# Attention and a gated expert layer on one core: queries and keys of the two heads on even and odd partitions, and every row block stored with its pair

## The chip, the cores and the metric

The kernel runs on one core of one Trainium2 chip. The metric is device time in microseconds (us) of one execution. A profile is one execution taken by the hardware profiler; its times are counted from the start of its span, which is the stretch from the first to the last instruction. TensorE is written PE, its weight load PEld, VectorE DVE, ScalarE ACT, GpSimd POOL and SyncE SP. SPq is the queue of instructions on SP, from which nearly all transfers are issued.

## The reference

The first half is attention inside chunks of 64 rows (8 batches, 8 heads, 576 rows of 64 numbers); the second half sends each of the 4608 rows of 512 numbers to one of 8 experts and keeps 80 rows for each.

```
scores = scale * q_c @ k_c^T              # per chunk of 64 rows
attn   = exp(scores - max); attn /= sum + 1e-9
x      = (attn @ v_c) as rows [4608, 512]
logits = x @ w_gate                       # 8 experts
e      = argmax(logits); gate = softmax(logits)[e]
for each expert: keep the 80 rows with the largest gate
    out[row] = gate * (relu(x[row] @ w1[e]) @ w2[e])
```

All other rows of the output are zero.

## The kernel before

**Stage one, attention.** The rows are cut into 36 blocks of 128 rows, two chunks of 64 each; two blocks make a pair, so there are 18 pairs (`n`), and four blocks make a tile `T` of 9. The loop over `n` is written out by hand: in step `n` PE does the scores of pair `n` (`scores`, tile `s`), turns the finished rows of pair `n-3` (`xtrans`, tile `px`), multiplies the probabilities of pair `n-2` with the values (`values`, tile `o`), turns the probabilities of pair `n-1` (`probs`, tile `pt`), and in even steps does the gate products (`gate_mm`) and, from step 8 on, a count (`tally`). DVE takes maxima and differences of pair `n` and then divides pair `n-2` (`divide`), which writes the finished rows into a tile of SBUF; `store` writes them to the scratch tensor `xs` in HBM.

**Queries and keys.** For each block, `load_qk` fills one of six buffers `qb` of 128 partitions and 1536 columns with two transfers of 64 partitions and 1024 columns (256 KB). One head lies on partitions 0 to 63, columns 0 to 1023; the other on 64 to 127, columns 512 to 1535. Columns 512 to 1023 are then the stationary operand, and columns 0 to 511 and 1024 to 1535 the moving one; the quarters that no head fills are set to zero once, at the start. So one matmul with 128 rows of contraction does both heads. The values go into six buffers `vb` by two transfers each of 130 KB (`load_v`), one head on the even partitions and the other on the odd ones: `vbufs[i % NBV][h:P:2, h]`.

**Rows kept on the chip.** Tiles 0, 2 and 4 (`KEEP`) are written into `kept`, which lies in the two weight buffers that the second expert's weights get later; the others into `x`, of which there are two. The kept tiles are stored whole (1 MB each) in steps 15, 16 and 17 (`DEFER`), after the last load of queries and keys. The others are stored pair by pair, right behind their division.

**The order of transfers.** SP issues transfers in program order, one after the other. Each waits for its buffer to be free and for the transfer issued eight before it to have landed. In steps 15 to 19 (`EARLY`) the weights of experts 0 and 1 are loaded in pieces of 1 MB; the last two wait for a small copy on POOL (L639).

**Stage two, choice of rows.** Behind the loop come the last pairs and gates, the threshold of each expert, and the list of rows. POOL then gathers 128 rows of `xs` at a time into `xgc` (L179), six gathers.

**Stage three, experts.** Two matrix products for each gathered group (`hc` L204, `yc` L237), with the weights of the other six experts and the zero rows of the output on the queue beside them.

Of the kernel before, what the change touches and what calls it, by code (L numbers as in the profile page):

```python
# [8 lines left out]
F32 = mybir.dt.float32  # L9
# [8 lines left out]
P = 128  # L18
# [8 lines left out]
DM = 512  # L27
# [9 lines left out]
LG = NT - 1  # L37
HOT = 8
OB = 171
KEEP = (0, 2, 4)  # L40
DEFER = {15: [0], 16: [2], 17: [4]}
LATER = [[(2, 1), (3, 0), (3, 1)], [(0, 2), (4, 0), (5, 0), (1, 2)], [(4, 1), (5, 1), (2, 2)], [(6, 0), (6, 1), (3, 2), (4, 2), (7, 0)], [(7, 1), (5, 2), (6, 2), (7, 2), (8, 2)], [], [], []]

EARLY = {15: [0], 16: [1], 17: [2, 3], 18: [4], 19: [5]}
# [13 lines left out]
def attention_moe(ctx: ExitStack, tc: tile.TileContext, qk, vv, wg, w1, w2, cap, cst, out):  # L58
# [3 lines left out]
    wp = ctx.enter_context(tc.tile_pool(name="weights", bufs=2))  # L62

    xs = dp.tile([NT * 512, DM], F32, name="xs")
# [219 lines left out]
    with ExitStack() as actx:  # L284
        gk = actx.enter_context(tc.tile_pool(name="gating", bufs=2, side="right"))
        wk = actx.enter_context(tc.tile_pool(name="work", bufs=2))
# [10 lines left out]
            return small[:, turn[0], 0:a * b].rearrange("p (a b) -> p a b", b=b)  # L297

        TT = {}
        kept = []  # L300
        QKV = {}
        XT = {}
        U = {}
# [8 lines left out]
        def pops(k):  # L312
            for _ in range(k):
                step_one(gates)
# [8 lines left out]
        def load_qk(i, eng=nc.sync):  # L323

            d = QKV["qk", i] = qbufs[i % (2 * NB)]
            for h in range(2):
                eng.dma_start(d[64 * h:64 * h + 64, 512 * h:512 * h + 1024],
                              qk[i // 2, i % 2, 64 * h:64 * h + 64])

        vbufs = [wk.tile([P, 2, VW], F32, name=f"vb{j}", tag=f"vb{j}", bufs=1)  # L330
# [2 lines left out]
        def load_v(i):  # L333
            for h in range(2):
                nc.sync.dma_start(vbufs[i % NBV][h:P:2, h], vv[i // 2, i % 2, h])  # L335

        def scores(n):
            d = U[n] = {}
            ps = d['s'] = ps1.tile([P, 2, 512], F32, name=f"s{n}", tag="o" if n == 1 else "s")
            for t in range(2):  # L340
                t8 = QKV["qk", 2 * n + t].rearrange("p (w a u s) -> p w a u s", w=3, a=4, u=2)
                for pr in range(4):
                    for u in range(2):
                        nc.tensor.matmul(  # L344
                            ps[64 * u:64 * u + 64, t, P * pr:P * pr + P].rearrange(
                                "p (h k) -> p h k", h=2),
                            lhsT=t8[:, 1, pr, u, :], rhs=t8[:, 0:3:2, pr, u, :],
                            start=True, stop=True)
# [31 lines left out]
        def values(i, tag=None):  # L380
            n, t = divmod(i, 2)
            T, r = divmod(i, 4)
            d = U[n]
            if r == 0:
                if T in KEEP:
                    k, j = divmod(KEEP.index(T), 2)
                    if j == 0:
                        kept.append(wp.tile([P, 8, DM], F32, name=f"kept{k}", tag=f"w{k + 1}"))
                    TT[T] = kept[k][:, 4 * j:4 * j + 4]
                else:  # L390
                    TT[T] = wk.tile([P, 4, DM], F32, name=f"x{T}", tag="x")
            v = vbufs[i % NBV].rearrange("p h (a u x) -> p h a u x", a=4, u=2)
            if tag is None:
                if t == 0:
                    d['o'] = ps1.tile([P, 3 * 512], F32, name=f"o{n}", tag="o")
                k0, po = 4 * t, d['o']
            else:
                k0, po = 0, ps1.tile([P, 2 * 512], F32, name=f"o{i}", tag=tag)
                U[i, 'o'] = po
            for pr in range(4):  # L400
                c, o = 64 * (4 * t + pr), OB * (k0 + pr)
                for u in range(2):
                    nc.tensor.matmul(  # L403
                        po[64 * u:64 * u + 64, o:o + 130].rearrange(
                            "p (h x) -> p h x", h=2),
                        lhsT=d['pT'][:, u, c:c + 64], rhs=v[:, :, pr, u, :],
                        start=True, stop=True)
# [11 lines left out]
                TT[T][:, r:r + nt, :].rearrange("p r (k h e) -> p (r k) h e", k=4, h=2),  # L419
                pov[..., 0:64], rc[:, :, :, None].to_broadcast([P, k, 2, 64]), op=ALU.mult)  # L420

        def store(n, nt=2):
            T, r = divmod(2 * n, 4)
            if T == 8:
                for u in range(2):
                    nc.sync.dma_start(
                        xs.rearrange("(b s) d -> s b d", s=576)[
                            512:576, 2 * r + u:2 * r + 4:2, :],
                        TT[T][64 * u:64 * u + 64, r:r + 2, :])
            else:  # L430
                nc.sync.dma_start(
                    xs[T * 576:T * 576 + 512].rearrange("(c p) d -> p c d", p=P)[:, r:r + nt],
                    TT[T][:, r:r + nt])

        def xtrans(n, tag="tp"):
            T, r = divmod(2 * n, 4)
# [26 lines left out]
        def gate_sum(T, queue):  # L463
            pm = bank([P, 4, 32])
            nc.tensor.transpose(pm.rearrange("p c e -> p (c e)"), U.pop(('lt', T)), ident)
            gate(4 * T, 4, pm[:, :, 0:NE], queue)
# [177 lines left out]
        with tc.manual_schedule():  # L644
            warm = gk.tile([P, 2 * P], BF16, name="warm", tag="lv", bufs=LV)
            nc.vector.memset(warm, 0.0)
            for j, qb in enumerate(qbufs):
                eng = nc.gpsimd if j == 1 else nc.vector
                eng.memset(qb[64:P, 0:512], 0.0)
                eng.memset(qb[0:64, 1024:1536], 0.0)  # L650
                if j < 2:
                    load_qk(j, (nc.sync, nc.scalar)[j])
            nc.scalar.dma_start(ident, cst[:, C_ID:C_ID + P])
# [5 lines left out]
            def warm_up(n):  # L659
                for j in range(n):  # L660
                    nc.tensor.matmul(pw, lhsT=warm[:, 0:P], rhs=warm, start=True, stop=True)
# [21 lines left out]
            def late_constants():  # L683
                for dst, c0, w in ((io_b, C_IO, 2 * P), (tr_b, C_TR, P)):
                    nc.scalar.copy(dst, ct[:, c0:c0 + w])
                io_h = S['io_h'] = gk.tile([P, P, HOT], BF16, name="io_h", tag="io_h", bufs=1)
                nc.gpsimd.tensor_copy(io_h, io_b[:, P:2 * P, None].to_broadcast([P, P, HOT]))
                nc.gpsimd.tensor_copy(capf, capi)
                nc.gpsimd.tensor_scalar(capc, capf[:, 0:1], 0.0, 4294967296.0,
                                        op0=ALU.is_lt, op1=ALU.mult)  # L690
                nc.gpsimd.tensor_tensor(capt, capf[:, 0:1], capc, op=ALU.add)
                nc.gpsimd.tensor_scalar(capc, capf[:, 1:2], 4294967296.0, None, op0=ALU.mult)
                nc.gpsimd.tensor_tensor(capt, capt, capc, op=ALU.add)
                nc.gpsimd.tensor_scalar(slot_oob, ct[:, C_SL:C_SL + NR], capt, BIG,
                                        op0=ALU.is_ge, op1=ALU.mult)

            for n in range(NPAIR):
                odd = n % 2
                if n == 2:
                    late_constants()  # L700
                scores(n)
                if n + NB < NPAIR:
                    load_qk(2 * (n + NB))
                    if n < 2:
                        load_qk(2 * (n + NB) + 1)
                if n >= 5 and odd:
                    gate_sum((n - 5) // 2, gates)
                if n >= 3:
                    xtrans(n - 3)
                if n >= 2:  # L710
                    for t in range(2):
                        values(2 * (n - 2) + t)
                        if n - 2 + NBV // 2 < NPAIR:
                            load_v(2 * (n - 2) + t + NBV)
                        if t == 0 and n + NB < NPAIR:
                            load_qk(2 * (n + NB) + 1)
                if n >= 1:
                    probs(n - 1)
                if n == 1:
                    warm_up(8)  # L720
                if n >= 7 and odd:
                    for j in range(2 * n - 14, 2 * n - 10):
                        signs(j)
                if n >= 8 and not odd:
                    tally(2 * n - 16, 4)
                if n >= 4 and not odd:
                    gate_mm((n - 4) // 2)
                    gate_copy((n - 4) // 2)
                maxima(n)
                minus(n)  # L730
                if n >= 2:
                    divide(2 * (n - 2), 2)
                    if (n - 2) // 2 not in KEEP:
                        store(n - 2)
                for T in DEFER.get(n, ()):
                    store(2 * T, 4)
                if n >= 8 and not odd:
                    left_add(2 * n - 16)
                if odd:
                    pops(6 if n >= 7 else 4)  # L740
                else:
                    pops(len(gates) - 2)
                if n == NPAIR - 2:
                    own_counts()
                for k in EARLY.get(n, ()):
                    early_weights(k)
# [335 lines left out]
```

## Time and profile before

| what | value |
| --- | --- |
| time, median of 3 runs | 274.38 us (274.06 to 275.83) |
| time of the profiled execution | 277.03 us |
| its span | 275.2 us |
| PE busy, DVE busy | 232.4 us, 119.0 us |
| moved by DMA | 84.73 MB, mean 308 GB/s |
| HBM read, written | 64.00 MB, 20.45 MB |

The profiled execution is 1.0% longer than the median. Mean rates hide that the rate of the DMA engines is not the same in the three stages; the rows further below take it stage by stage.

### The profile page before, as it was taken

How to read it: one execution, taken by the hardware profiler on the slowest of the kernel's cores; microseconds unless marked ns; L12 is line 12 of the kernel's file. 1: busy time of each engine (PE TensorE's matmuls, PEld its weight loads, DVE VectorE, ACT ScalarE, POOL GpSimd, SP SyncE). 2: the span in 40 equal slices, each digit the busy share in tenths (PEclk: the TensorE clock that was granted, in tenths of full speed). 3: DMA queues.
4: the chain of work that ended last, by engine and by line, in shares of the span. 5: the costliest groups of instructions: out<-in, count | busy, mean ns of one | idle time of the engine just before them, and what ended most of it. 6: DMA issues, size and time to landing. Idle time of an engine off the chain costs nothing.

```text
span 275.2 us, 7328 instructions
## 1 busy us (share of the span) xinstructions
PE 232.4 (84%) x3117; PEld 149.7 (54%) x3117; DVE 119.0 (43%) x263; ACT 66.5 (24%) x115; POOL 57.0 (21%) x167
## 2 busy tenths in 40 slices
PE   6773989979788977978868885899999999999990
PEld 4763778968667866766756574234333433333320
DVE  6545366876574846665735846011111211212110
ACT  1012123453251625352614410112020201101000
POOL 8003000121122222222373845300000000000081
PEclk9599799999999999999979779599999999999996
DMA  7998999999999999999999999999999999999431
GB/s 157 237 255 220 233 239 238 274 257 260 232 239 284 288 230 215 276 271 272 365 394 402 409 411 415 393 396 393 409 413 405 407 415 409 416 395 409 182 133 69
DMA packets 35718, 84.73 MB, mean 308 GB/s; under 512 B 4000, under 2 KB 4128, under 8 KB 35680
## 3 DMA queue, kind: packets, MB, share of 16 engines
q1 hardware_dynamic: 34416, 80.73, 93.0%
q0 software_dynamic: 960, 2.88, 2.7%
q10 hardware_dynamic: 304, 0.59, 1.0%
q8 instruction: 27, 0.44, 0.7%
q14 instruction: 11, 0.09, 0.1%
HBM read 64.00 MB, written 20.45 MB: 307 GB/s over the span
## 4 chain that ended last, share of the span: by engine, by line
PE 51%; DMA 39%; SPq 3%; POOL 3%; issue 2%; POOLq 0%; DVE 0%
DMA qb<-in_qk 24%; PE hc L204 16%; PE yc L237 15%; DMA vb<-in_vv 5%; PE o L403 5%; PE s L344 5%; DMA xs<-kept 4%; DMA w<-in_w 4%; DMA xgc<-xs,gic 2%; PE hpc L222 2%; SPq L335 2%; PE pt L369 2%; PE px L369 1%; PE xpc L192 1%; PE small L455 1%
## 5 line engine op out<-in xcount | busy, mean ns | idle before, releaser
L344 PE MATMUL s<-qb 128*64 128x128 f32 x576 | 42.3, 298 | 21.7 <-DMA qb<-in_qk 20.0
L344 PEld LDWEIGHTS s<-qb 128*64 128x64 f32 x576 | 35.6, 150 | 27.0 <-issue 22.4
L204 PE MATMUL hc<-w,xtc 128*32 128x512 f32 x384 | 45.6, 618 | 0.0
L237 PE MATMUL yc<-w,htc 128*32 128x512 f32 x384 | 42.3, 592 | 0.0
L403 PE MATMUL o<-vb,pT 128*64 128x130 f32 x576 | 38.0, 283 | 3.3 <-DMA vb<-in_vv 2.6
L354 DVE TENSOR_REDUCE mx<-s 128x16 f32<-128x1024 f32 x18 | 22.0, 1225 | 36.8 <-PE s L344 36.7
L403 PEld LDWEIGHTS o<-vb,pT 128*64 128x64 f32 x576 | 33.1, 139 | 4.8 <-issue 3.7
L237 PEld LDWEIGHTS yc<-w,htc 128*32 128x32 f32 x384 | 12.4, 110 | 28.3 <-issue 28.3
L204 PEld LDWEIGHTS hc<-w,xtc 128*32 128x32 f32 x384 | 12.6, 113 | 27.3 <-issue 26.7
L446 ACT COPY xT<-px 128x1024 f32<-128x1024 f32 x17 | 17.2, 1013 | 42.3 <-PE px L369 42.3
L378 ACT ACTIVATE pT<-pt 128x1024 f32<-128x1024 f32 x18 | 18.4, 1023 | 32.1 <-PE pt L369 32.1
L256 POOL DMA_INDIRECT out<-ysc,to x6 | 6.0, 993 | 88.5 <-SPq L933 86.1
L359 DVE TENSOR_TENSOR sm<-s,mx 128x1024 f32<-128x1024 f32 x18 | 22.1, 1228 | 0.6
L209 ACT ACTIVATE hsc<-hc 128x512 f32<-128x512 f32 x6 | 3.6, 597 | 65.3 <-PE hc L204 65.3
L242 DVE TENSOR_SCALAR ysc<-yc,gatec 128x512 f32<-128x512 f32 x6 | 4.5, 751 | 33.5 <-PE yc L237 33.5
L418 DVE TENSOR_TENSOR x<-o,rc 128x1024 f32<-128x1024 f32 (+1 forms) x14 | 15.0, 1072 | 0.5
L211 DVE TENSOR_SCALAR hsc<-hc 128x512 f32<-128x512 f32 x6 | 4.1, 691 | 25.2 <-PE hc L204 25.2
L520 POOL TENSOR_SCALAR u<-sx 128x4 f32<-128x4 f32 x8 | 1.6, 195 | 62.1 <-DVE sx L519 38.9
L369 PE MATMUL pt<-ct,sm 64*128 64x64 f32 x288 | 12.8, 229 | 1.2 <-ACT pT L378 1.2
L226 DVE COPY htc<-hpc 128x512 f32<-128x512 f32 x6 | 4.2, 692 | 22.0 <-PE hpc L222 22.0
L369 PEld LDWEIGHTS pt<-ct,sm 64*128 64x128 f32 x288 | 10.3, 139 | 4.3 <-issue 3.0
L545 ACT ACTIVATE lv<-io_b,bo 128x256 bf16<-128x256 bf16 x29 | 12.5, 497 | 0.4 <-DVE bo L526 0.4
(136 smaller groups left out, 233.8 us busy)
## 6 DMA issues: line engine op xcount, KB each, us to landing
w<-in_w SPq DMA_DIRECT2D x12, 2048.0 KB, 18.8
qb<-in_qk SPq DMA_DIRECT2D x70, 256.0 KB, 6.7
vb<-in_vv SPq DMA_DIRECT2D x72, 130.0 KB, 6.6
out<-zero SPq DMA_DIRECT2D x9, 1024.0 KB, 16.3
w<-in_w SPq DMA_DIRECT2D x8, 1024.0 KB, 12.6
xs<-x SPq DMA_DIRECT2D x10, 512.0 KB, 6.5
xs<-kept SPq DMA_DIRECT2D x3, 1024.0 KB, 8.8
xs<-x SPq DMA_DIRECT2D x4, 256.0 KB, 10.7
```

The costliest lines, as they stand in the source:

```text
L204: nc.tensor.matmul(h[o:o + 32, :], lhsT=xT[r][:, b, o:o + 32], rhs=getw(groups[r][g])[0][:, b, 512 * f:512 * f + 512], start=(b == 0), sto ...
L237: nc.tensor.matmul(y[o:o + 32, :], lhsT=hT[r][c // 4][:, c % 4, o:o + 32], rhs=getw(groups[r][g])[1][:, c, :], start=(c == 0), stop=(c == ...
L256: i = nc.gpsimd.indirect_dma_start(out=out, out_offset=bass.IndirectOffsetOnAxis(ap=to, axis=0), in_=ys, in_offset=None, bounds_check=NT * ...
L344: nc.tensor.matmul(ps[64 * u:64 * u + 64, t, P * pr:P * pr + P].rearrange("p (h k) -> p h k", h=2), lhsT=t8[:, 1, pr, u, :], rhs=t8[:, 0:3 ...
L354: nc.vector.tensor_reduce(d['mx'], d['s8'], axis=AX.X, op=ALU.max)
L359: nc.vector.tensor_tensor(d['sm'].rearrange("p c k h -> p h c k"), d['s8'], d['mx'][:, :, :, None].to_broadcast([P, 2, 8, 64]), op=ALU.sub ...
L369: nc.tensor.transpose(pm[:, u, 64 * c:64 * c + 64], src(c)[rows], ident[rows, rows])
L378: nc.scalar.activation(d['pT'], pt, AF.Exp, scale=0.125)
L403: nc.tensor.matmul(po[64 * u:64 * u + 64, o:o + 130].rearrange("p (h x) -> p h x", h=2), lhsT=d['pT'][:, u, c:c + 64], rhs=v[:, :, pr, u, ...
L418: nc.vector.tensor_tensor(TT[T][:, r:r + nt, :].rearrange("p r (k h e) -> p (r k) h e", k=4, h=2), pov[..., 0:64], rc[:, :, :, None].to_br ...
L446: nc.scalar.copy(dst, pm)
L545: nc.scalar.activation(lv, io_b, AF.Sign, bias=bo[:, rt:rt + 1], scale=-1.0)
```

## The change

Queries and keys of one head go to the even partitions and those of the other to the odd ones, as the values do already; what is in HBM and the columns stay as they were. Since the empty quarters now lie on every second partition, the zeros are written over all 128 partitions of the two column ranges before the loads, so the first load of each buffer writes over zeros and waits for them. No tile is kept: all nine go through the two buffers `x`, and all 18 pairs are stored behind their division, 512 KB at a time.

```diff
-KEEP = (0, 2, 4)
-DEFER = {15: [0], 16: [2], 17: [4]}
...
             for h in range(2):
-                eng.dma_start(d[64 * h:64 * h + 64, 512 * h:512 * h + 1024],
+                eng.dma_start(d[h:P:2, 512 * h:512 * h + 1024],
                               qk[i // 2, i % 2, 64 * h:64 * h + 64])
...
             if r == 0:
-                if T in KEEP:
-                    k, j = divmod(KEEP.index(T), 2)
-                    if j == 0:
-                        kept.append(wp.tile([P, 8, DM], F32, name=f"kept{k}", tag=f"w{k + 1}"))
-                    TT[T] = kept[k][:, 4 * j:4 * j + 4]
-                else:
-                    TT[T] = wk.tile([P, 4, DM], F32, name=f"x{T}", tag="x")
+                TT[T] = wk.tile([P, 4, DM], F32, name=f"x{T}", tag="x")
...
                 eng = nc.gpsimd if j == 1 else nc.vector
-                eng.memset(qb[64:P, 0:512], 0.0)
-                eng.memset(qb[0:64, 1024:1536], 0.0)
+                eng.memset(qb[:, 0:512], 0.0)
+                eng.memset(qb[:, 1024:1536], 0.0)
...
                     divide(2 * (n - 2), 2)
-                    if (n - 2) // 2 not in KEEP:
-                        store(n - 2)
-                for T in DEFER.get(n, ()):
-                    store(2 * T, 4)
+                    store(n - 2)
```

The order of instructions on PE and ACT is the same in both kernels; on DVE and POOL only the memsets have another shape; on SP six stores are added and three taken out. The names in the rows are tiles with a buffer number; `waits` names the counters that an instruction waits for, `DMAHW` for an earlier transfer, `DVE`, `Pool` and `PE` for work of that engine.

SP at the start of the program, before:

```order
L327 DMA qb_99<-in_qk 64x1024 x2
L327 DMA qb_101<-in_qk 64x1024 x2
L327 DMA qb_102<-in_qk 64x1024
L327 DMA qb_102<-in_qk 64x1024 [waits DMAHW0_49]
L335 DMA vb_105<-in_vv 64x520 [waits DMAHW1_49,DVE_49]
```

The same place on SP after the change:

```order
L324 DMA qb_99<-in_qk 64x1024 [waits DVE_49] x2
L324 DMA qb_101<-in_qk 64x1024 [waits DVE_49] x2
L324 DMA qb_102<-in_qk 64x1024 [waits DVE_49]
L324 DMA qb_102<-in_qk 64x1024 [waits DMAHW0_49,DVE_49]
L332 DMA vb_105<-in_vv 64x520 [waits DMAHW1_49,DVE_49]
```

Nothing moved, but the loads of queries and keys now wait for DVE's memsets of their buffers.

SP in the middle of the loop, from the loads of the first reused buffers on, before:

```order
L335 DMA vb_105<-in_vv 64x520 x2
L327 DMA qb_104<-in_qk 64x1024 x2
L335 DMA vb_106<-in_vv 64x520 x2
L327 DMA qb_99<-in_qk 64x1024 x2
L335 DMA vb_107<-in_vv 64x520 x2
L327 DMA qb_100<-in_qk 64x1024 x2
L335 DMA vb_108<-in_vv 64x520 x2
```

The same place on SP after the change:

```order
L332 DMA vb_105<-in_vv 64x520 x2
L324 DMA qb_104<-in_qk 64x1024 x2
L332 DMA vb_106<-in_vv 64x520 x2
L422 DMA xs<-x_299 128x2x512
L324 DMA qb_99<-in_qk 64x1024 x2
L332 DMA vb_107<-in_vv 64x520 x2
L324 DMA qb_100<-in_qk 64x1024 x2
L332 DMA vb_108<-in_vv 64x520 x2
L422 DMA xs<-x_299 128x2x512
```

A store that waits for DVE's division now stands ahead of the next pair's loads in every step, where before it stood there only for tiles that were not kept.

SP at the end of the loop, before:

```order
L431 DMA xs<-x_1668 128x2x512
L431 DMA xs<-kept_299 128x4x512
L640 DMA w_0_1875<-in_w 128x2x1024
L335 DMA vb_109<-in_vv 64x520 x2
L335 DMA vb_110<-in_vv 64x520 x2
L431 DMA xs<-x_1914 128x2x512
L431 DMA xs<-kept_299 128x4x512
```

The same place on SP after the change:

```order
L422 DMA xs<-x_1675 128x2x512
L631 DMA w_0_1881<-in_w 128x2x1024
L332 DMA vb_109<-in_vv 64x520 x2
L332 DMA vb_110<-in_vv 64x520 x2
L422 DMA xs<-x_1920 128x2x512
```

The stores of the kept tiles are gone from between the last loads of values.

## Rows read from the trace of the kernel before

**Rows 1.** The chain that ended last, from the page: shares by engine, by line.
```profile
PE 51%; DMA 39%; SPq 3%; POOL 3%; issue 2%; POOLq 0%; DVE 0%
DMA qb<-in_qk 24%; PE hc L204 16%; PE yc L237 15%; DMA vb<-in_vv 5%; PE o L403 5%; PE s L344 5%; DMA xs<-kept 4%; DMA w<-in_w 4%; DMA xgc<-xs,gic 2%; PE hpc L222 2%; SPq L335 2%; PE pt L369 2%; PE px L369 1%; PE xpc L192 1%; PE small L455 1%
```

**Rows 2.** List of waits, whole span: total us, times, longest us.
```profile
PE s L344 <- DMA qb<-in_qk: 20.0, 12, 4.7
```

**Rows 3.** Stretches: length, busy of each engine, clock granted, DMA share, GB/s last.
```profile
11.80:12.80 1.00, 1.00 (x13) 1.00 (x12) 0.73 (x1) 0.00 (x0) 0.00 (x0) 0.50 1.05 193
12.80:13.80 1.00, 1.00 (x14) 1.00 (x12) 0.96 (x2) 0.00 (x0) 0.00 (x0) 0.50 1.07 376
14.00:18.00 4.00, 3.23 (x50) 2.67 (x48) 3.01 (x3) 1.02 (x1) 0.00 (x0) 0.96 1.07 229
28.00:128.00 100.00, 87.22 (x1630) 75.15 (x1627) 64.36 (x117) 39.04 (x61) 16.00 (x72) 0.98 1.05 253
139.00:152.00 13.00, 9.50 (x151) 7.89 (x151) 5.39 (x25) 4.66 (x11) 6.77 (x17) 0.87 1.04 404
170.00:250.00 80.00, 77.29 (x680) 27.34 (x684) 10.49 (x20) 9.94 (x18) 4.20 (x5) 0.96 1.04 405
```

**Rows 4.** DMA view of two stretches: 12.9 to 13.7 us, then 14 to 18.
```profile
DMA packets 179, 0.31 MB, mean 382 GB/s; under 512 B 33, under 2 KB 33, under 8 KB 179
DMA packets 272, 0.92 MB, mean 229 GB/s; under 512 B 48, under 2 KB 48, under 8 KB 272
```

**Rows 5.** Timeline of PE in the loop: start, us, instructions, idle ahead of them.
```profile
30.07 1.70 PE L344 MATMUL s<-qb 128*64 128x128 f32 x16 [0.38 <-DMA qb<-in_qk]
...
47.72 1.97 PE L344 MATMUL s<-qb 128*64 128x128 f32 x32
...
50.25 2.00 PE L403 MATMUL o<-vb,pT 128*64 128x130 f32 x32
...
53.83 1.97 PE L344 MATMUL s<-qb 128*64 128x128 f32 x32
...
59.20 1.09 PE L344 MATMUL s<-qb 128*64 128x128 f32 x16
...
66.15 0.35 PE L565 MATMUL small<-mine,lv 128*128 128x8 bf16 x8
...
98.58 1.85 PE L344 MATMUL s<-qb 128*64 128x128 f32 x27 [1.43 <-issue]
...
129.22 1.09 PE L344 MATMUL s<-qb 128*64 128x128 f32 x16 [1.24 <-DMA qb<-in_qk]
```

**Rows 6.** Timeline of DVE and SP in one step: a division, the next store.
```profile
47.68 1.22 DVE L418 TENSOR_TENSOR x<-o,rc 128x1024 f32<-128x1024 f32 x1
...
51.30 0.38 SPq L431 DMA_DIRECT2D xs<-x  x1
```

**Rows 7.** Timeline at the start, SP and DVE; then landing times of qb.
```profile
0.73 4.06 SPq L327 DMA_DIRECT2D qb<-in_qk  x6
...
1.78 0.48 DVE L650 MEMSET qb<- 64x512 f32 x1
...
8.47 2.41 SPq L335 DMA_DIRECT2D vb<-in_vv  x4
...
23.00 6.30 SPq L327 DMA_DIRECT2D qb<-in_qk  x10
...
DMA to landing us min/median/max: 3.5/6.7/9.1
```

**Rows 8.** Timeline behind the loop: last values, POOL, first gather, first expert matmuls.
```profile
141.24 3.32 PE L403 MATMUL o<-vb,pT 128*64 128x130 f32 x32 [2.57 <-DMA vb<-in_vv]
...
152.31 0.39 POOL L639 COPY w<-bo 128x1 f32<-128x1 f32 x2 [0.61 <-DMA xs<-kept]
...
166.06 1.30 POOL L179 DMA_INDIRECT xgc<-xs,gic  x1 [4.81 <-DVE bt L852]
...
172.68 1.09 PE L192 MATMUL xpc<-ct,xgc 128*128 128x128 f32 x4 [3.62 <-DMA xgc<-xs,gic]
```

More of the change, by code (lines that the diff above doesn't have):

```diff
@@ L299, in attention_moe @@
         TT = {}
-        kept = []
         QKV = {}
@@ L420, in divide, with store @@
                 pov[..., 0:64], rc[:, :, :, None].to_broadcast([P, k, 2, 64]), op=ALU.mult)
-        def store(n, nt=2):
-            T, r = divmod(2 * n, 4)
+        def store(n):
+            T, r = divmod(2 * n + 1, 4)
             if T == 8:
@@ L427, in store @@
                         xs.rearrange("(b s) d -> s b d", s=576)[
-                            512:576, 2 * r + u:2 * r + 4:2, :],
-                        TT[T][64 * u:64 * u + 64, r:r + 2, :])
+                            512:576, 2 * r - 2 + u:2 * r + 2:2, :],
+                        TT[T][64 * u:64 * u + 64, r - 1:r + 1, :])
             else:
                 nc.sync.dma_start(
-                    xs[T * 576:T * 576 + 512].rearrange("(c p) d -> p c d", p=P)[:, r:r + nt],
-                    TT[T][:, r:r + nt])
+                    xs[T * 576:T * 576 + 512].rearrange("(c p) d -> p c d", p=P)[:, r - 1:r + 1],
+                    TT[T][:, r - 1:r + 1])
         def xtrans(n, tag="tp"):
```

## The prediction

> **What bounds the kernel now.** The chain that ended last comes first: half of it is PE and 39% DMA, and of the DMA share 24% is one transfer, the loads of queries and keys [rows 1]. Where a chain names a transfer, the list of waits says who stood still: PE waited 12 times and 20.0 us in all for these loads in front of the scores [rows 2]. The expert products stand in the same chain with 16% and 15% [rows 1] and are PE's own work.
>
> The table by stretch then says what limits the transfers. Over the loop (28 to 128 us) the DMA engines are full (share 1.05) and move 253 GB/s; from 139 to 152 us they are just as full and move 404, and among the experts 405 [rows 3]. So the loop is limited by engines that are busy but slow. Two short stretches before the loop say which transfers are slow. From 14 to 18 us the rate is 229 GB/s: 48 of its 272 packets are small, so 0.92 MB in 224 large ones is 4.1 KB each, the row of a query and key load (1024 numbers of 4 bytes). From 12.9 to 13.7 us 0.31 MB in 146 large packets is 2.1 KB each, the row of a value load (520 numbers), at 382 GB/s [rows 4]. The loads whose head takes 64 neighbouring partitions run at little more than half the rate of those that take every second one. The slow start of the values is to be seen too: 193 GB/s in the first microsecond, then 376 [rows 3].
>
> **The change part by part.** *The rate.* A pair moves four loads of 256 KB, four of 130 KB and a store of 512 KB, 2056 KB or 2.11 MB, once all stores stand in the loop. At 253 GB/s that is 8.3 us, at 376 it is 5.6, at 404 it is 5.2. The trace has no load of queries and keys on every second partition, so its price has two ends: 253, if nothing is gained, and 404. I take 376, from the row whose transfers have the same pattern of partitions; its slow first microsecond comes when a new kind of transfer begins, and I count it as an uncertainty of the loop.
>
> [...]
>
> *The loop.* With 5.6 us per pair for DMA, PE is next. In the stretch where nothing keeps it waiting, a step with gate products takes 53.83 - 47.72 = 6.11 us and one without 59.20 - 53.83 = 5.37 [rows 5]; from step 8 the count adds 0.28 (it starts at 66.15 and takes 0.35, of which some lies under its neighbours). From pair 3 to pair 17 there are fourteen steps: seven of 5.37, two of 6.11, five of 6.39, together 81.8 us. PE also pauses for no reason that the profile shows, once for 1.43 us [rows 5]; I add 3.2 for the loop, two or three such pauses. So 85.0 us, 6.07 per pair. Before, the second half of the scores starts at 30.07 for pair 3 and at 129.22 for pair 17 [rows 5], 99.15 us. The loop gives 14.1 us.
>
> *Stores in every step.* SP issues nine transfers per pair where a kept tile had eight. Four in a row take 2.41 us and ten 6.30 [rows 7], 0.6 each, so 5.4 us per pair: under 6.07, with little to spare. The store waits for the division, and the next pair's loads stand behind it. The division ended at 48.90 [rows 6], 1.2 us after the next scores had begun at 47.72 and before they end (1.97 us long [rows 5]); the first load behind the store needs the first half of those scores anyway. I cost the wait at nothing, hidden by PE; without that cover it is up to 1 us per step. DVE's work is the same.
>
> *Memsets.* The first load waited for nothing and was issued at 0.73; now it waits until DVE's second memset ends at 1.78 + 0.48 = 2.26 [rows 7], 1.5 us later. The same memset over 128 partitions in place of 64 has no row; I take the same time, since its columns are the same, and twice the time (0.5 us more for each) as the other end. The cover is SP: its next transfers, the values, are issued from 8.47 on in both kernels, because they wait for memsets of their own. From there to the last load of pair 3 it issues 12 loads of values, 8 of queries and keys and 3 of constants, 23 in all, at 0.6 each: 13.8 us, so 22.3, and with 3.5 us at least to landing [rows 7] 25.5 us. Against 30.07 that gives 4.6 us. If the transfers are no faster, the 1.5 us is lost instead.
>
> *Behind the loop.* The last products with values waited 2.57 us for a load and took 3.32 us [rows 8] where 32 of them take 2.00 [rows 5]. These loads are queued behind kept stores and weights on a full queue; with fewer transfers left over both go, 3.9 us. POOL waited 0.61 us for a kept store in front of the copy at 152.31 [rows 8], but its second copy needs the last count's input at about the same time, so I take nothing. The first gather took from 166.06 to 172.68 until PE could start [rows 8], on full engines. With the backlog smaller I take 1.5 us off, between 0 and 3.5 (a landing of about 3, as the shortest in the loads' row).
>
> *The experts.* PE works there for 77.29 of 80 us [rows 3]. They move as a block, unless weights now land late: nothing is moved into this stage.
>
> Sum: 4.6 + 14.1 + 3.9 + 1.5 = 24.1 us off. The profiled execution took 277.03 us (span 275.2), so one like it would take 252.9. The median of the timed runs is 274.38; since no part of the sum depends on the 2.65 us between them, I take the same sum from it: **250.3 us**.
>
> **The rivals.** *Size, not place (slower).* The loads stay as slow as they are: the 16 engines that write every second partition may meet at the same places just as now. The row at 193 GB/s is that case [rows 3], and it lasted a microsecond. Then six stores of 512 KB, 3.15 MB, move into the loop at 253 GB/s: 12.4 us more. They leave the stage behind the loop, which gives back 3.9 at most, and the memsets take 1.5: 274.4 + 10.0 = 284.4. It decides below about 2.11 x 14 / (99.15 + 3.9) = 287 GB/s. For it speaks that the loads are small; against it, that value loads half as large ran at 376.
>
> [...]
>
> *DMA stays the bound, but faster.* If the meeting of engines recurs at every change between kinds of load, the mean of 193 and 376 is 285, and with stores, which write nothing to SBUF, some 310: 6.8 us per pair, 95 for the loop. Then 4 + 3 + 3.9 + 1 = 12: 262.4.
>
> *SP becomes the bound.* If the waits for divisions add to the 5.4 us of issue, say 1 us, a pair takes 6.4 and the loop 89.6; the sum is 4.6 + 9.6 + 3.9 + 1.5 = 19.6, so 254.8.
>
> *The gain is given back to the experts.* DMA is full there at 405 GB/s [rows 3]. If the 4 MB of weights that are loaded early slid behind the gather, they would cost 10 us: 260. Against it: from the end of the loop to the gather there are over 30 us, 12 MB at 404, for 10 MB.
>
> **How the numbers follow.** Forecast 0.62, DMA still the bound 0.17, SP 0.10, given back 0.04, slower 0.05, no change (gain and added stores cancel, near 287 GB/s) 0.02. Faster by over 1% is 0.93, within 1% (about what a measurement of this kernel can tell from no change) 0.03, slower 0.04 (the slower rival counts 0.05, of which 0.01 falls within 1%). The range: at the fast end no pauses (3.2), two more us at the start, 2 at the gather and the rest as above, 243; at the slow end the DMA rival with its price a little worse, 264.
>
> **What would show it.** Right: in the loop the GB/s rise to about 340 with a DMA share under 1, PE's waits for these loads nearly vanish, pair 3's scores stand near 25 us and pair 17's near 110, the first gather near 142. The first loads alone would run near 376 or more. Wrong: a DMA share still over 1 in the loop with under 300 GB/s, or rows of the loads at the old rate; SP without idle time and the loads landing in front of their use would mean the SP rival; idle PE in front of `hc` or `yc` would mean that weights are late.

## The result, and the profile after

| what | before | after |
| --- | --- | --- |
| time, median of 4 runs each | 274.69 us (274.06 to 275.83) | 260.52 us (258.75 to 262.44) |
| time of the profiled execution | 277.03 us | 259.46 us |
| its span | 275.2 us | 257.7 us |
| PE busy, moved by DMA | 232.4 us, 84.73 MB | 227.0 us, 84.73 MB |

The ratio is 0.948 (0.940 to 0.957): 14.2 us less. That lies in the range and on the forecast side, but 10.2 us above the forecast of 250.3. The two profiled executions differ by 17.6 us, since the one of before ran 2.3 us above its median and the one of after 1.1 below.

From the page of the changed kernel: three engines in 40 slices of 6.4 us, and the chain that ended last [rows 1].

```profile
PE   6851999999999988798878858999999999999990
...
DMA  5868999999999989999999998999999999999240
GB/s 206 282 217 243 365 346 327 308 326 320 304 311 334 315 293 317 310 318 295 332 405 413 410 392 281 401 393 411 416 409 401 416 408 413 410 397 404 111 156 36
...
PE 68%; DMA 10%; SPq 9%; DVE 4%; POOL 3%; issue 3%; ACT 0%; POOLq 0%; DVEq 0%
PE hc L202 17%; PE yc L235 16%; PE o L394 10%; PE s L341 9%; DMA qb<-in_qk 5%; SPq L332 5%; PE px L366 4%; SPq L324 3%; PE small L446 3%; PE pt L366 3%; DMA vb<-in_vv 3%; DMA xgc<-xs,gic 2%; PE hpc L220 2%; PE xpc L190 1%; DVE qb L641 1%
```

The loads of queries and keys had 24% of the chain and have 5%; PE went from 51 to 68%. SP's queue has grown in it from 3% to 9%: the issuing of loads, not their transfer.

Stretches of the same kernel: the first loads alone, the whole loop, and the rows of the list [rows 3] that stand for start, loop, and the gather.

```profile
2.60:7.00 4.40, 3.18 (x27) 2.38 (x27) 3.85 (x9) 1.63 (x3) 3.74 (x8) 1.00 0.97 352
...
14.00:18.00 4.00, 2.26 (x38) 2.05 (x40) 0.03 (x1) 0.00 (x0) 0.00 (x0) 1.00 0.78 256
...
28.00:116.00 88.00, 84.65 (x1630) 74.63 (x1626) 64.44 (x117) 38.73 (x61) 16.73 (x75) 0.98 0.95 321
...
140.00:150.00 10.00, 8.86 (x86) 7.65 (x83) 5.79 (x25) 1.86 (x7) 4.91 (x8) 0.80 1.04 413
```

The first of these stretches in the kernel before:

```profile
2.60:7.00 4.40, 2.80 (x19) 1.95 (x17) 3.35 (x8) 1.28 (x1) 3.85 (x8) 1.00 1.01 225
```

From 2.6 to 7 us queries and keys are on their way, and in the changed kernel 64 KB of constants beside them: 352 GB/s, where the old pattern gave 225, and 229 from 14 to 18 us [rows 3]. The loop moves 321 GB/s in place of 253 and the DMA share is 0.95, no longer over 1. From 14 to 18 us the engines are not even busy (0.78), and PE stands still for 1.7 of the 4 us: there something else is late.

It is SP. Its timeline in the changed kernel, at the start and then for one pair in the loop (71.76 to 78.25), with the stores of some others (start, us, instructions):

```profile
1.55 3.78 SPq L324 DMA_DIRECT2D qb<-in_qk  x6
...
7.51 2.39 SPq L332 DMA_DIRECT2D vb<-in_vv  x4
9.95 4.12 SPq L324 DMA_DIRECT2D qb<-in_qk  x4
14.17 2.46 SPq L332 DMA_DIRECT2D vb<-in_vv  x4
...
20.88 6.29 SPq L324 DMA_DIRECT2D qb<-in_qk  x10
...
31.12 0.53 SPq L422 DMA_DIRECT2D xs<-x  x1
...
58.33 0.53 SPq L422 DMA_DIRECT2D xs<-x  x1
...
64.29 1.34 SPq L422 DMA_DIRECT2D xs<-x  x1
...
71.76 0.53 SPq L422 DMA_DIRECT2D xs<-x  x1
72.39 1.39 SPq L324 DMA_DIRECT2D qb<-in_qk  x2
73.87 1.18 SPq L332 DMA_DIRECT2D vb<-in_vv  x2
75.11 1.23 SPq L324 DMA_DIRECT2D qb<-in_qk  x2
76.43 1.72 SPq L332 DMA_DIRECT2D vb<-in_vv  x2
78.25 0.53 SPq L422 DMA_DIRECT2D xs<-x  x1
...
112.01 0.53 SPq L422 DMA_DIRECT2D xs<-x  x1
```

Behind each row of that pair the next begins within 0.1 us. From 31.12 to 112.01 there are twelve pairs, so SP takes 80.89 / 12 = 6.74 us for the nine transfers of one, 0.75 each.

Is it the issuing, or does SP wait for the transfer issued eight before? In the kernel before that wait is there, as SP's list of waits from 28 to 130 us has it:

```profile
SPq L327 <- DMA qb<-in_qk: 17.7, 30, 1.2
```

In the changed kernel the list from 40 to 112 us names PE and DVE, and no transfer. By the landing times in its trace, each of SP's 87 issues from 40 to 105 us begins after the transfer eight before it has landed, in the median 1.45 us after. So it isn't landings that hold SP up there. PE's own timeline and its waits in front of the scores show what follows from it:

```profile
25.77 3.73 PE L341 MATMUL s<-qb 128*64 128x128 f32 x32 [5.43 <-DMA qb<-in_qk]
...
62.80 1.97 PE L341 MATMUL s<-qb 128*64 128x128 f32 x32
...
74.57 1.97 PE L341 MATMUL s<-qb 128*64 128x128 f32 x32
...
93.96 1.09 PE L341 MATMUL s<-qb 128*64 128x128 f32 x16 [0.83 <-DMA qb<-in_qk]
...
108.45 1.09 PE L341 MATMUL s<-qb 128*64 128x128 f32 x16 [1.62 <-DMA qb<-in_qk]
...
113.99 1.97 PE L341 MATMUL s<-qb 128*64 128x128 f32 x32
...
125.29 1.99 PE L394 MATMUL o<-vb,pT 128*64 128x130 f32 x32 [0.97 <-DMA vb<-in_vv]
...
155.47 1.09 PE L190 MATMUL xpc<-ct,xgc 128*128 128x128 f32 x4 [3.54 <-DMA xgc<-xs,gic]
```

```profile
PE s L341 <- DMA qb<-in_qk: 12.9, 8, 5.4
```

Undisturbed, PE needs (74.57 - 62.80) / 2 = 5.88 us per pair, less than SP's 6.74. So the loads, fetched three pairs ahead, lose ground by 0.86 us per pair. Until 92 us the lead covers that; then PE waits four times, 3.35 us in all. Before it waited 20.0 us in 12 waits [rows 2].

Piece by piece, from the two profiled executions: the scores of pair 3 end at 29.50 (31.77 before, [rows 5]), 2.3 us gained; from there to the end of pair 17's scores at 115.96 it takes 86.46 us (98.54 before), 12.1 gained; from there to the first gather at 148.93 (166.06 before, [rows 8]) 2.8 gained; from the gather to the first expert products 6.54 us (6.62 before), 0.1 gained; and behind them 0.3. Together 17.5, the difference of the spans. A second profile of the kernel before (the last experiment) shows that such a piece is known to about 2 us.

### The profile page after: what moved, and what is told of

Its sections match the earlier page's. It is cut to its first block, busy times and chain, and to the rows that moved or that the text cites. A ratio compares the mean times of both kernels' runs of the same rounds, so it can differ in the third digit from the quotient of the medians.

```text
span 257.7 us, 7341 instructions
## 1 busy us (share of the span) xinstructions
PE 227.0 (88%) x3117; PEld 145.5 (56%) x3117; DVE 118.7 (46%) x263; ACT 66.2 (26%) x115; POOL 56.9 (22%) x167
## 2 busy tenths in 40 slices
DMA packets 35766, 84.73 MB, mean 329 GB/s; under 512 B 4048, under 2 KB 4176, under 8 KB 35728
## 4 chain that ended last, share of the span: by engine, by line
PE 68%; DMA 10%; SPq 9%; DVE 4%; POOL 3%; issue 3%; ACT 0%; POOLq 0%; DVEq 0%
PE hc L202 17%; PE yc L235 16%; PE o L394 10%; PE s L341 9%; DMA qb<-in_qk 5%; SPq L332 5%; PE px L366 4%; SPq L324 3%; PE small L446 3%; PE pt L366 3%; DMA vb<-in_vv 3%; DMA xgc<-xs,gic 2%; PE hpc L220 2%; PE xpc L190 1%; DVE qb L641 1%
## 5 line engine op out<-in xcount | busy, mean ns | idle before, releaser
L341 PE MATMUL s<-qb 128*64 128x128 f32 x576 | 38.1, 284 | 13.1 <-DMA qb<-in_qk 12.9
L341 PEld LDWEIGHTS s<-qb 128*64 128x64 f32 x576 | 32.7, 141 | 16.8 <-issue 10.7
L394 PE MATMUL o<-vb,pT 128*64 128x130 f32 x576 | 36.4, 278 | 1.0 <-DMA vb<-in_vv 1.0
L394 PEld LDWEIGHTS o<-vb,pT 128*64 128x64 f32 x576 | 31.9, 136 | 2.2 <-PE px L366 1.1
L235 PEld LDWEIGHTS yc<-w,htc 128*32 128x32 f32 x384 | 12.4, 110 | 28.3 <-issue 28.3
L202 PEld LDWEIGHTS hc<-w,xtc 128*32 128x32 f32 x384 | 12.1, 114 | 27.8 <-issue 27.4
L409 DVE TENSOR_TENSOR x<-o,rc 128x1024 f32<-128x1024 f32 (+1 forms) x20 | 22.4, 1118 | 0.7
L366 PE MATMUL px<-ct,x 64*128 64x64 f32 x288 | 13.2, 234 | 0.0
## 6 DMA issues: line engine op xcount, KB each, us to landing
w<-in_w SPq DMA_DIRECT2D x12, 2048.0 KB, 17.6
```

What stands on the lines that cost most here:

```text
L202: nc.tensor.matmul(h[o:o + 32, :], lhsT=xT[r][:, b, o:o + 32], rhs=getw(groups[r][g])[0][:, b, 512 * f:512 * f + 512], start=(b == 0), sto ...
L235: nc.tensor.matmul(y[o:o + 32, :], lhsT=hT[r][c // 4][:, c % 4, o:o + 32], rhs=getw(groups[r][g])[1][:, c, :], start=(c == 0), stop=(c == ...
L341: nc.tensor.matmul(ps[64 * u:64 * u + 64, t, P * pr:P * pr + P].rearrange("p (h k) -> p h k", h=2), lhsT=t8[:, 1, pr, u, :], rhs=t8[:, 0:3 ...
L366: nc.tensor.transpose(pm[:, u, 64 * c:64 * c + 64], src(c)[rows], ident[rows, rows])
L394: nc.tensor.matmul(po[64 * u:64 * u + 64, o:o + 130].rearrange("p (h x) -> p h x", h=2), lhsT=d['pT'][:, u, c:c + 64], rhs=v[:, :, pr, u, ...
L409: nc.vector.tensor_tensor(TT[T][:, r:r + nt, :].rearrange("p r (k h e) -> p (r k) h e", k=4, h=2), pov[..., 0:64], rc[:, :, :, None].to_br ...
```

## The experiments

All of them compute the whole output; where something is added, the text says what. Ratios are to the kernel before, run on the same chip. "Q" and "V" are two theories on merged transfers, explained where they come up.

**The layout alone.** The changed kernel, with tiles 0, 2 and 4 kept on the chip again.

```diff
+KEEP = (0, 2, 4)
+DEFER = {15: [0], 16: [2], 17: [4]}
...
-                    store(n - 2)
+                    if (n - 2) // 2 not in KEEP:
+                        store(n - 2)
+                for T in DEFER.get(n, ()):
+                    store(2 * T, 4)
```

> The partition layout alone (with its memsets), rows of tiles 0, 2 and 4 still kept and stored late. Theory P (the place of the rows on the partitions sets the rate of the query and key loads, the stores weigh little): nearly the whole gain, 258 to 263 us, ratio 0.94 to 0.96, loop rate above 300 GB/s. Theory S (the gain comes from spreading the stores over the loop): near 274 us, ratio 0.99 to 1.01.

259.04 us, ratio 0.945 (0.936 to 0.955). **The stores alone** is the other half: the kernel before with no tile kept, its loads as they were.

```diff
-KEEP = (0, 2, 4)
-DEFER = {15: [0], 16: [2], 17: [4]}
...
-                    if (n - 2) // 2 not in KEEP:
-                        store(n - 2)
-                for T in DEFER.get(n, ()):
-                    store(2 * T, 4)
+                    store(n - 2)
```

> The stores alone (all rows stored pair by pair, nothing kept), queries and keys as before on neighbouring partitions. Theory P: 3.15 MB more go through a loop that stays at about 253 GB/s, so slower, 280 to 286 us, ratio 1.02 to 1.04. Theory S: most of the gain, 260 to 266 us.

277.16 us, ratio 1.009 (1.005 to 1.013), under the 280 to 286 us that were expected. So the layout makes the whole gain, and the stores cost 2.5 us with the slow loads and nothing that shows with the fast ones. Stretch 28 to 100 us of the kernel with the layout alone, then of the one with the stores alone:

```profile
28.00:100.00 72.00, 72.00 (x1414) 63.82 (x1412) 55.75 (x99) 32.88 (x52) 13.97 (x62) 0.99 0.92 297
```

```profile
28.00:100.00 72.00, 64.00 (x1147) 55.70 (x1142) 44.93 (x77) 26.56 (x40) 9.47 (x42) 0.93 1.04 275
```

With the layout alone PE is busy for all of this stretch and asks for no more than 297 GB/s, a little under the 300 expected. Its loop, taken as above from the end of pair 3's scores to the end of pair 17's, is 82.3 us against 86.5 with every store in it; behind the loop, where the kept tiles are stored, it needs 35.9 us against 33.0. So the stores cost time in the loop with the fast loads too, and most of it comes back behind the loop.

With the slow loads and six stores more in the loop the full engines move 275 GB/s in place of 253. The slower rival charged the 3.15 MB at 253, 12.4 us; at the 404 of [rows 3] they would be 7.8. The loop of this kernel takes 100.3 us, 1.8 more than in the first profile of the kernel before and 3.7 more than in the second. So the stores, which read SBUF, seem to have run in part beside the slow loads, which write it; no run shows that by itself. Some 5 us are saved behind the loop, and 2.5 us is the cost of the whole.

**Place or size.** The kernel before, whose loads stay on 64 neighbouring partitions, but with one load of 512 KB for the two blocks of a pair in place of two of 256 KB.

```diff
+            for h in range(2):
+                nc.sync.dma_start(
+                    qpair[n % NB][64 * h:64 * h + 64, :, 512 * h:512 * h + 1024],
+                    qk[n, :, 64 * h:64 * h + 64].rearrange("t p c -> p t c"))
...
-                    load_qk(2 * (n + NB))
...
+                    load_pair(n + NB)
...
```

> The kernel before, with the queries and keys of both blocks of a pair in one transfer per head: two of 512 KB in place of four of 256 KB, still on 64 neighbouring partitions. Theory P: the rate of the loop stays between 230 and 270 GB/s and the time between 270 and 278 us. Theory Z (the size of the transfers sets the rate): the loop's rate rises above 300 GB/s and the time falls to 262 to 268 us.

281.80 us, ratio 1.029 (1.019 to 1.039), with this stretch:

```profile
28.00:100.00 72.00, 61.27 (x1148) 53.64 (x1148) 45.00 (x77) 26.96 (x41) 9.49 (x42) 0.96 1.05 249
```

Twice the size leaves the rate at 249 GB/s on full engines. Size isn't the cause; the place is. The time lies above the 270 to 278 us expected. In the profile the loop is as long as before (98.5 us), but pair 3's scores begin 3.2 us later (30.97 against 27.81), so the loss arises at the start. That a block's scores wait there for the load of the whole pair is likely, but not shown.

**Fewer transfers to issue.** The changed kernel, with the values of the two blocks of a pair in one transfer per head (260 KB in place of 130): seven transfers per pair for SP, the same bytes.

```diff
-                nc.sync.dma_start(vbufs[i % NBV][h:P:2, h], vv[i // 2, i % 2, h])
+                nc.sync.dma_start(vbufs[i // 2 % (NBV // 2)][h:P:2, :, h],
+                                  vv[i // 2, :, h].rearrange("t p x -> p t x"))
...
```

> The changed kernel, with the values of both blocks of a pair in one transfer per head: two transfers of 260 KB in place of four of 130 KB, so SP issues 7 transfers per pair and not 9; bytes, layout and rates stay. Theory Q (SP's time per issue, some 0.6 to 0.75 us, paces the loop: 6.74 us per pair from store to store against 5.88 of PE): the waits for loads late in the loop (3.4 us) vanish and pair 3's loads are issued 3 us earlier, so 254 to 257 us. Theory R (the DMA engines, at a share of 0.95, are the limit): no change, 259 to 262 us.

248.18 us, ratio 0.903 (0.895 to 0.911), well under the 254 to 257 us that Q had. Its PE waits for these loads, the stretch, and the scores of pairs 3 and 17:

```profile
PE s L342 <- DMA qb<-in_qk: 3.3, 5, 1.5
```

```profile
28.00:100.00 72.00, 70.10 (x1372) 61.79 (x1370) 53.82 (x97) 32.31 (x51) 13.97 (x62) 1.00 1.00 366
```

```profile
22.12 2.33 PE L342 MATMUL s<-qb 128*64 128x128 f32 x32 [0.48 <-DMA qb<-in_qk]
...
106.75 1.97 PE L342 MATMUL s<-qb 128*64 128x128 f32 x32
```

The rate is 366 GB/s, the waits are down from 12.9 to 3.3 us. Piece by piece the profiled executions of this kernel and the changed one lie 8.9 us apart: 5.0 are gained up to the end of pair 3's scores, 2.2 in the loop, 0.7 behind it, 1.8 at the gather, and 0.8 are lost after it. So most of it does not come from the loop. Ahead of pair 3's loads SP has six transfers fewer, 3.6 us at 0.6 each; the scores begin 3.65 us earlier, and behind a wait of 0.48 us in place of 5.43 they take 2.33 us in place of 3.73.

But two readings fit: SP's issue time was missing (Q), or value transfers of twice the size run faster (V). **Both merged**, queries and keys too (five transfers per pair):

```diff
...
+                nc.sync.dma_start(
+                    qpair[n % NB][h:P:2, :, 512 * h:512 * h + 1024],
+                    qk[n, :, 64 * h:64 * h + 64].rearrange("t p c -> p t c"))
...
```

> The changed kernel with values and also queries and keys of a pair in one transfer per head: 5 transfers per pair on SP. Theory Q (SP's time per issue was what the changed kernel lost): 7 transfers per pair already leave PE as the bound, so nothing more is gained, 246 to 251 us; the loads of a pair now wait for the whole pair before, which may cost up to 2 us. If SP still limited at 7, it falls to 243 to 246 us.

248.88 us, ratio 0.903 (0.896 to 0.910): no more to be had, PE is busy for 72.00 of the 72 us from 28 to 100. **Merged values in the kernel before**, its loads slow and its tiles kept, with the edit of the values as above:

> The kernel before (queries and keys on neighbouring partitions, tiles kept) with the values of a pair in one transfer per head. If SP's issues had limited that kernel too, it would gain like the changed one, 262 to 266 us. If its DMA engines did, at the slow rate, 272 to 277 us and the loop's rate stays between 245 and 265 GB/s.

270.16 us, ratio 0.984 (0.975 to 0.994), between the two expectations: a gain of 4 us at 262 GB/s on full engines, where the changed kernel gains 12. It doesn't tell Q from V.

**One more issue.** The changed kernel with a transfer of 1 KB behind each of the 16 stores, which nobody reads: ten to issue per pair, and next to no bytes.

```diff
                     store(n - 2)
+                    junk = wk.tile([P, 2], I32, name=f"junk{n}", tag="junk", bufs=8)
+                    nc.sync.dma_start(junk, cap[0:1, :].broadcast_to([P, 2]))
```

> The changed kernel with one more transfer of 1 KB (8 bytes to each partition) behind every store, 16 in all: the output stays the reference's. Theory Q: SP spends 0.4 to 0.6 us more per pair on its issue, 7.2 us in place of 6.74, and falls behind sooner: 5 to 8 us slower than the changed kernel, 265 to 268 us. Theory R (DMA engines are the limit): 16 KB more are nothing, 259 to 262 us.

269.42 us, ratio 0.976 (0.966 to 0.985): 8.9 us over the changed kernel by the medians and 7.5 by the two ratios, so near or above the upper end of what Q had. From its timeline of SP:

```profile
38.17 0.53 SPq L422 DMA_DIRECT2D xs<-x  x1
38.74 0.47 SPq L726 DMA_DIRECT2D junk<-in_cap  x1
...
112.23 0.54 SPq L422 DMA_DIRECT2D xs<-x  x1
```

74.06 us for ten pairs, 7.41 each, 0.74 per transfer. The loop is 8.2 us longer than in the changed kernel. The DMA share falls to 0.89 while PE's waits for queries and keys grow to 15.6 us: the engines idle and SP doesn't.

**The other merge, and the merge undone in count.** To settle Q against V: the changed kernel with only queries and keys merged (edit as in the kernel with both), so the value transfers stay at 130 KB and SP has seven to issue;

> The changed kernel, but the queries and keys of a pair in two transfers of 512 KB in place of four of 256 KB; the values stay four of 130 KB, so SP issues seven transfers per pair, as with merged values alone (which measured 248). Theory Q (SP's issue time is what the changed kernel lacked): the loop is PE-bound again, some 85 us, and the time 247 to 252. Theory V (the gain of the merged values came from value transfers of twice the size): the value transfers are as small as in the changed kernel, so 258 to 262.

and the kernel with merged values, with two transfers of 1 KB behind each store, so the large transfers stay and SP has nine again:

```diff
                     store(n - 2)
+                    for _ in range(2):
+                        junk = wk.tile([P, 2], I32, name=f"junk{n}", tag="junk", bufs=8)
+                        nc.sync.dma_start(junk, cap[0:1, :].broadcast_to([P, 2]))
```

> The changed kernel with merged values (248 measured), and two more transfers of 1 KB behind each store, so that SP issues nine per pair again while the data moved are the same but for 2 KB per pair. Theory Q: two issues of 0.47 us take SP to some 6.2 to 6.7 us per pair, over PE's 5.9; PE waits for queries and keys late in the loop and the time is 253 to 260. Theory V: the value transfers keep their size, so 247 to 250.

The first: 251.01 us, ratio 0.911 (0.904 to 0.918), as Q had it. The second: 262.95 us, ratio 0.954 (0.946 to 0.963), some 14 us over the kernel that it was made from, and above Q's own range; V is excluded by both. A wider theory, that larger transfers of either kind run faster, would survive the first; the second contradicts it, and so does the kernel with one more issue. Between the second's profile and that of the kernel with merged values 6.9 of 15.1 us lie in the loop, and most of the rest behind it, which neither theory had priced. Stores of the first, on SP, then of the second:

```profile
35.32 0.54 SPq L431 DMA_DIRECT2D xs<-x  x1
...
97.82 0.54 SPq L431 DMA_DIRECT2D xs<-x  x1
```

```profile
35.03 0.54 SPq L424 DMA_DIRECT2D xs<-x  x1
...
71.91 1.51 SPq L727 DMA_DIRECT2D junk<-in_cap  x2
...
112.50 0.52 SPq L424 DMA_DIRECT2D xs<-x  x1
```

Eleven pairs each: 5.68 us per pair, about PE's own pace, and 7.04, which is 0.78 per transfer. The second kernel's profiled execution took 265.68 us, 1% over its median.

**A second queue.** The changed kernel, with the second head's value loads issued by ACT, to relieve SP without any change of sizes.

```diff
-                nc.sync.dma_start(vbufs[i % NBV][h:P:2, h], vv[i // 2, i % 2, h])
+                (nc.sync, nc.scalar)[h].dma_start(vbufs[i % NBV][h:P:2, h], vv[i // 2, i % 2, h])
```

> The changed kernel with the value load of the second head issued by ACT and that of the first by SP: every transfer keeps its size and place, SP issues 7 per pair and not 9, ACT two. Theory Q (SP's time per issue): 248 to 253 us, most of what merging the value loads gave. If merging helped because the transfers got larger (theory V), 258 to 262 us. ACT waits for nothing new of weight, since its next work needs a later matmul than the load does; if it delays ACT all the same, the time rises by up to 2 us.

Its executions spread from 269.77 to 279.77 us, and no ratio was settled; both theories missed. SP's waits in the profiled one (276.55 us), the stretch, and one transfer of SP behind two of ACT:

```profile
SPq L324 <- DMA vb<-in_vv: 29.3, 10, 5.5
SPq L332 <- DMA vb<-in_vv: 12.8, 7, 5.3
```

```profile
28.00:100.00 72.00, 63.07 (x1127) 55.23 (x1128) 44.65 (x77) 26.15 (x40) 9.40 (x42) 0.92 0.79 256
```

```profile
78.23 1.37 ACTq L332 DMA_DIRECT2D vb<-in_vv  x2
81.06 0.47 SPq L324 DMA_DIRECT2D qb<-in_qk  x1
```

SP now stands still for 42 us, waiting for value loads. Each transfer waits for the one issued eight before it, and in the program's order those eight include transfers that ACT issues, behind its other work, as the two from 78.23 ahead of SP's load at 81.06. SP's issue work went down, but a new wait took its place, so this says nothing on Q or V.

**Before, once more**, for the spread of the profiles:

> The kernel before, once more with a profile, to see how much the stretches of one kernel differ from profile to profile: pair 17's scores at 129 to 131 us and the first gather at 164 to 167 us if the first profile was typical; earlier by 2 to 3 us if its 277.03 us against a median of 274.7 lies in these stretches.

276.64 us (span 274.8), with the first gather at 165.37 us, 0.7 us from the first profile. Pair 17's scores end at 129.06 (130.31 in the first), and the loop takes 96.6 us (98.5). So a place in the profile of before is known to about a microsecond, and the length of a piece to about two.

## Why the prediction was right, and where it was off

**The bound and its cause: right.** The loads' place on the partitions sets their rate (352 GB/s for the first ones, 225 in the same stretch before; twice the size changes nothing), and the layout alone makes the whole gain. The price taken from the value loads, 376 GB/s, was good: with SP relieved the loop runs at 366 to 372. What makes neighbouring partitions slower is shown by no run.

**The step that failed: "Stores in every step".** SP's issue was put at 5.4 us per pair, 0.6 for each transfer, and at no cost, since PE was to take 6.07. It is 6.74 against PE's 5.88. The price came from the shortest rows; the first six loads take 4.06 us in [rows 7], 0.68 each, and at that nine make 6.1, which no longer hides behind PE. The prediction had a rival in which SP becomes the bound, with waits for divisions as its cause, and 254.8 us. The place was right, the cause wasn't: SP's waits for DVE from 40 to 112 us come to 1.2 us in all, so what was said of the division, "hidden by PE", held. The nine issues themselves are longer than 0.6. Durations of the loads in the pair quoted, from the view of the tiles `qb` and `vb` from 71.7 to 78.3 us (min/median/max in ns):

```profile
L324 SPq DMA_DIRECT2D qb<-in_qk x4: 472/592/862, 72.4 to 75.7; - x4
...
L332 SPq DMA_DIRECT2D vb<-in_vv x4: 546/590/1078, 73.9 to 77.6; - x4
```

Most take 0.47 to 0.60 us, and in every pair one to three take 0.75 to 1.7; with what lies between the rows that makes 5.96 us for the shortest pairs (58.33 to 64.29) and 6.74 in the mean. The list of waits puts the long ones down to PE, 8.3 us from 40 to 112. For the longest one of this pair, issued at 76.43 for values, that doesn't fit. The products that last read its buffer, those of pair 7, were these:

```profile
65.60 2.00 PE L394 MATMUL o<-vb,pT 128*64 128x130 f32 x32
```

They had ended 8.8 us before. What makes such issues long stays open. Large transfers aren't needed for it: a pair of added 1 KB transfers, 0.47 us for one, took 1.51. SP is late at the start already: from 14 to 18 us the DMA share is 0.78, and with merged values pair 3's scores begin 3.65 us earlier. With two transfers per pair less, the time is 248.2 to 251.0, which is what the forecast said for a kernel in which SP costs nothing.

Against the 4.8 us that a load of queries and keys takes in the median from issue to landing, 0.75 us is small. But transfers overlap here, while each issue begins within 0.1 us of the end of the one before it (the pair quoted), so it has to be set against the 0.74 us that 256 KB take at 352 GB/s, and there it isn't small.

**The terms.** *Start*, 4.6 forecast, 2.3 measured. The memsets cost 0.8, not 1.5 (first load issued at 1.55, before at 0.73), and a memset over 128 partitions takes 0.48 us, as over 64 [rows 7]:

```profile
1.04 0.48 DVE L640 MEMSET qb<- 128x512 f32 x1
```

The sum itself has a slip: 22.3 and 3.5 are 25.8, not 25.5, so the term should have been 4.3. The 23 issues took 15.8 us (from 7.51 to 23.3) and not 13.8, and the last load of pair 3 landed 4.6 us after its issue, at 27.4, where 3.5 had been taken. Pair 3's scores begin at 25.77, where the second half of them was forecast at 25.5; they follow a wait of 5.43 us and run at a granted clock of 0.50: 3.73 us in place of 1.97. *Loop*, 14.1 forecast, 12.1 measured: the four late waits of 3.35 us are SP's. The 3.2 us set aside for pauses were not needed, since the loop shows none that nothing explains, so one took the other's place and the miss is only 2.0. That is luck. *Behind the loop*, 3.9 forecast, 2.8 measured; a wait of 0.97 us for the last values stayed, of the 2.57 [rows 8], and the products take 1.99 us in place of 3.32. *Gather*, 1.5 forecast, 0.1 measured: the engines are as full as before (share 1.04, 413 GB/s); from 138 to 150 us a load of weights of 2 MB is issued there. That makes 17.3 of 24.1; *experts* 0, measured 0.3.

In the kernel with merged values the same pieces are 7.3 (start), 14.3 (loop), 3.5 (behind the loop), 1.8 (gather) and -0.5 (experts). So, as far as 2 us can tell, all terms but the start came out as forecast once SP had less to issue. That speaks for the working of the sum, and for SP as what it lacked.

**The base.** The sum was taken from the median, though it was read from an execution 2.7 us above it. The terms miss 6.6 us between the profiles (24.1 less 17.5), and the two profiled executions lie 3.4 us farther apart than the medians: together 10.0 of the 10.2 us by which the forecast was low.

**The rivals.** *Size, not place* falls by the kernel with 512 KB on neighbouring partitions, and its price for the stores by the kernel with the stores alone. *DMA stays the bound* came nearer in time (262.4) than the forecast, but not in cause: the share is under 1 (0.95) and fewer issues alone give 10 to 12 us. *Given back to the experts* didn't occur: they take the same time within 0.3 us. That engines meet at the same places, which two of the rivals rest on, was the author's supposition; no run shows it.

The version to keep has merged values as well: 248.18 us, 0.903 of before.

## What to carry to other kernels

When a transfer gets faster, count what its queue has to issue per step with the same care as bytes and matmuls, from the period of a repeated instruction in the loop rather than from the shortest rows, and compare it with the engine that will be next. A load of 64 partitions was not slow here once its rows lay on every second partition (352 GB/s, against 225 on neighbours), and one transfer for two blocks costs one issue in place of two. Before a second queue is used to relieve the first, look at which landings each of its instructions waits for.

## What was not expected of the hardware

The time of an issue on SP hardly depended on what was moved: 0.47 us for 1 KB, 0.53 for a store of 512 KB, and mostly 0.54 to 0.60 for loads of 256 KB. One transfer more per pair lengthened SP's period by 0.67 us (6.74 to 7.41).

Full engines moved 275 GB/s (share 1.04) with six stores more in the loop and 253 (share 1.05) without, and the loop grew by 1.8 to 3.7 us, where the stores' bytes alone would be 7.8 us at 404 GB/s. That the stores ran in part beside the slow loads is a reading of these figures, which no run shows by itself.

Behind a wait of 5.43 us on PE the 32 matmuls took 1.76 us more than their usual 1.97, at a granted clock of 0.50; the waits of 0.83 and 1.62 us late in the loop were followed by 16 matmuls at 1.09 us, the usual time.
